# Windowed attention in fp32 by head pairs, one head in each row half of TensorE's array, with a new priority table for the list scheduler

## The chip, the cores and the metric

The kernel runs on one core of a Trainium2 chip. The metric is the device time of one execution in microseconds (us); the kernel before has a median of 611.61 us over three runs (611.47 to 611.87).

## The reference, cut to what matters

Three stages follow each other. The change is in the first one and in the order of all three.

```python
# q, k, v: 4 batches x 8 heads x 576 positions x 64
scores = q @ k.T / 8 - slope[h] * |rel|      # rel = query position - key position
scores = where((rel >= 0) & (rel < 128), scores, -1e9)
attn = softmax(scores)                       # exp, sum, divide by (sum + 1e-9)
x = attn @ v                                 # heads side by side: 4 x 576 x 512
# stage 2, gMLP: h = gelu(x @ w_in), halves u and v; v = layernorm(v);
#   x = x + (u * (w_sg @ v + b_sg)) @ w_out
# stage 3, RWKV channel mix: out = sigmoid(xr @ w_r) * (relu(xk @ w_k)^2 @ w_v)
#   xk, xr: mixes of each position with the one before it
```

All inputs and results are fp32 (the weights of the two later stages arrive as 64 bit words and are decoded on the chip).

## The kernel before, in words

**Attention.** A query tile is 128 positions; because of the window it needs 256 keys, the first tile 128. A head has four whole tiles (i = 0 to 3) and a last one of 64 queries (i = 4). `s_bank` computes score tiles into PSUM, two tiles to a bank, and the tag `s` has two banks. Heads 0 to 7 (`PLAIN_S`) multiply in fp32, with the contraction of 64 padded to all 128 rows of the array; the trace writes each fp32 matmul as two MATMUL passes. Heads 8 to 31 use fp32r instead: `prep_head` splits q and k into a rounded part and a rest (tiles QK and KL), both parts of q lie one above the other in the 128 rows, and two fp32r matmuls (`s<-QK`, `s<-KL,QK`) make a tile. `s_tile` adds the mask and takes the row maximum on DVE (one custom operation out of PSUM, the tile p and nmax), ACT takes the exponential with its sum, and after a head's last tile the sums are inverted (sum, rin) and the five tiles are scaled on DVE, POOL or ACT.

Then p is transposed on TensorE. From head `FOLD` = 16 on, a tile's two key halves are first added, so that four transposes do (`tf`), and `keep` takes the triangles apart again afterwards; the last queries of two heads take two more with 64 rows (`tf4`). Heads 0 to 15 need seven transposes of 128x128 and three small ones with 64 rows (`t`). `av_step` multiplies v by a pair's transposed tiles: one head in each column half of the array (64 columns each, `a<-pf,rawv`). The last 64 queries follow apart in `a4_step`, whose matmuls go into the half empty bank of a later head's last score tile (`s<-pf,rawv`). Copies to x and the split into xg (a cast and a subtraction for each 128 of 512 columns) end the stage.

**gMLP** (`moe1`) makes v tiles (5 x 12 matmuls, `d<-w_in_t,xg`), u tiles (`d<-xg,w_in_t`), the position mix (`d<-w_sg_t,vhl`) and the output (`d<-gg,w_out_t`), all in fp32r in three passes over split operands. `merge` interleaves batch b's gMLP with batch b+1's attention; the first batch's attention has nothing to lie under, so a first stretch ends where the first `d` matmul starts. There, matmuls of constant data (`wps<-tri`, `K.filler`) stand where the planner expects TensorE to wait. Stage 3 (`phase2`: `d<-xk,wk`, `rps`, `vps`) follows.

**What sets the order.** Every operation is recorded with its estimated cost on each engine that may do it. `Rec.rank` gives it a latest start, and the table `PRI` shifts that by the label of the written tile and the engines; `Rec.schedule` is a list scheduler that runs the engines against these numbers, chooses the engine (biases in `ENG`) and so writes out each engine's fixed instruction order, DMA issues on SP among them. Nothing is reordered at run time.

Of the kernel before, what the change touches and what calls it, by code (L numbers as in the profile page):

```python
# [20 lines left out]
P = 128  # L21
# [12 lines left out]
    ("vsg", "dve"): -4000, ("w_in_t", "act/dve/pool"): 33000, ("w_sg_t", "act/dve/pool"): -17000, ("x", "act/dve"): 4000, ("xg", "dve/pool"): -13000,  # L34
}
ENG = {
    ("KL", "dve/pool", "pool"): 68000, ("QK", "act/dve", "dve"): 17000, ("QK", "dve/pool", "dve"): 43500, ("p", "dve/pool", "dve"): -2000,
    ("p", "dve/pool", "pool"): -14000, ("p", "dve/pool/act", "act"): 1000, ("p", "dve/pool/act", "dve"): 45000, ("pf", "act/dve", "dve"): 5000,
    ("pf4", "act/dve", "act"): -36000, ("vhl", "act/dve/pool", "dve"): 13000, ("w_in_t", "dve/pool", "dve"): 2000,
    ("w_out_t", "dve/pool", "dve"): -19000, ("w_sg_t", "act/dve/pool", "dve"): -9000, ("wk", "dve/pool", "dve"): 17000,  # L40
    ("xg", "dve/pool", "dve"): 4000,
}
NWARM = 10
FOLD = 16
FM = (1, 1)


def EARLY(n, i):
    return False


PLAIN_S = (0, 1, 2, 3, 4, 5, 6, 7)
PLAIN_A = range(32)
ODD = (1, 3, 5, 7)
# [72 lines left out]
class Op:  # L127
    __slots__ = ("i", "alts", "deps", "outs", "indeg", "ready", "lst", "nominal", "rdy", "start", "end", "eng", "lat", "key", "lab", "cnt", "astart", "aend", "abusy", "w0", "pe", "port")


class Rec:
# [9 lines left out]
    SPAN, DUTY = 3400.0, 0.7  # L141
# [55 lines left out]
    def link(self, nbufs):  # L197
        ops = self.ops
        self.nb = nbufs
        for (pool, tag), tl in self.tags.items():  # L200
# [3 lines left out]
            for k in range(1, len(tl)):  # L204
# [6 lines left out]
                if prev is not first:  # L211
                    first.deps.add(prev)
# [7 lines left out]
        for o in ops:  # L220
            o.outs = []
# [311 lines left out]
def attn_gmlp_rwkv_kernel(  # L533
# [91 lines left out]
    def plain_s(n):  # L625
        return n in PLAIN_S

# [648 lines left out]
```

## Time and profile before

| | |
|---|---|
| median of 3 runs | 611.61 us (611.47 to 611.87) |
| the profiled execution: its own time, its span | 611.09 us, 609.4 us |
| PE busy in the span | 594.2 us (98%) |
| DVE, ACT, POOL busy | 453.1 us (74%), 340.1 us (56%), 204.3 us (34%) |
| chain that ended last | PE 81%, DVE 11%, ACT 5% |
| granted TensorE clock, mean | 0.999 |

The span runs from the first instruction to the last. A matmul's record is longer than the time that it takes up in a stream, since matmuls are pipelined: what one costs is the distance between the starts of two neighbours, and the text uses that throughout.

### The profile page before, as it was taken

The page shows a single profiled execution, that of the slowest core. Times are in us where ns is not written, and L with a number is a line of the kernel's source. Part 1 is how long each engine was busy: PE and PEld are TensorE (multiplying, and loading weights), DVE is VectorE, ACT ScalarE, POOL GpSimd, SP SyncE. Part 2 cuts the span into 40 slices and gives each one's busy share as a digit, 9 for nine tenths or more (in the row PEclk, how much of TensorE's full clock was granted, in tenths as well). Part 3 has the DMA queues.
Part 4 walks back from the last instruction along what each step waited for, and adds up shares of the span by engine and source line. Part 5 has one row for each costly group of instructions (what it writes and reads, how often), then busy time and mean ns, then how long its engine had stood idle before and what let it go on. Part 6 is the DMA issues. An engine that isn't in the chain of part 4 may idle for free.

```text
span 609.4 us, 10294 instructions
## 1 busy us (share of the span) xinstructions
PE 594.2 (98%) x3593; PEld 502.9 (83%) x3593; DVE 453.1 (74%) x1199; ACT 340.1 (56%) x859; POOL 204.3 (34%) x348
## 2 busy tenths in 40 slices
PE   8898999999999999999999999999999999999997
PEld 4566889998789997899889988787888887888896
DVE  5989999899999889988498998892592249226122
ACT  5898888686777767874166456532521432234031
POOL 5587672437667555673053330000000001000000
PEclk9999999999999999999999999999999999999999
DMA  8974413325131323100352427414002000000100
GB/s 305 331 214 143 154 59 98 120 89 200 40 101 54 124 65 137 40 23 13 112 207 70 139 93 268 134 35 122 17 18 86 1 0 37 34 2 0 53 18 34
DMA packets 25332, 57.74 MB, mean 95 GB/s; under 512 B 4416, under 2 KB 13120, under 8 KB 24768
## 3 DMA queue, kind: packets, MB, share of 16 engines
q1 hardware_dynamic: 25280, 57.09, 28.4%
q8 instruction: 28, 0.46, 0.3%
q14 instruction: 24, 0.20, 0.1%
HBM read 47.63 MB, written 9.45 MB: 94 GB/s over the span
## 4 chain that ended last, share of the span: by engine, by line
PE 81%; DVE 11%; ACT 5%; issue 1%; DMA 1%; POOL 0%; SPq 0%; DVEq 0%; ACTq 0%; POOLq 0%
PE d L398 46%; PE vps L398 15%; PE rps L398 7%; PE s L398 6%; PE a L398 4%; PE t L406 2%; PE tf L406 2%; ACT p L420 1%; ACT wdec L591 1%; DVE p L718 1%; DVE wdec L476 1%; DVE w_v_t L440 1%; DVE mt L476 1%; DMA rawqk<-in_qk_dram 1%; ACT p L503 1%
## 5 line engine op out<-in xcount | busy, mean ns | idle before, releaser
L398 PE MATMUL d<-xk,wk 128*128 128x512 f32 (+1 forms) x480 | 105.3, 368 | 0.0
L398 PEld LDWEIGHTS d<-xk,wk 128*128 128x128 f32 x480 | 84.7, 188 | 16.1
L398 PE MATMUL vps<-w_v_t,k2h 128*128 128x512 f32 x288 | 94.1, 396 | 0.3 <-DVE r L440 0.3
L420 ACT ACTIVATE p<-p,nmax 128x256 f32<-128x256 f32 (+3 forms) x160 | 76.6, 480 | 27.5 <-DVE nmax L718 26.9
L420 ACT ACTIVATE rl<-d 128x512 f32<-128x512 f32 (+1 forms) x40 | 22.1, 554 | 81.2 <-PE d L398 76.4
L398 PE MATMUL d<-w_sg_t,vhl 128*128 128x288 f32 x448 | 66.4, 298 | 0.0
L398 PEld LDWEIGHTS vps<-w_v_t,k2h 128*128 128x128 f32 x288 | 54.2, 188 | 13.7 <-DVE r L440 1.0
L718 DVE CUSTOM_DVE_ANT_0 p<-s,mask 128x256 f32<-128x256 f32 (+3 forms) x160 | 60.1, 381 | 6.8 <-PE s L398 6.2
L398 PEld LDWEIGHTS d<-w_sg_t,vhl 128*128 128x128 f32 x448 | 60.8, 188 | 0.7 <-issue 0.2
L398 PE MATMUL d<-w_in_t,xg 128*128 128x512 f32 (+1 forms) x240 | 61.2, 399 | 0.0
L398 PE MATMUL vps<-w_v_t,k2l 128*128 128x512 f32 x144 | 57.0, 396 | 0.0
L430 DVE CAST k2h<-rl 128x512 fp32r<-128x512 f32 (+1 forms) x31 | 12.1, 391 | 59.9 <-ACT rl L448 59.8
L398 PE MATMUL d<-xg,w_in_t 128*128 128x288 f32 x384 | 56.7, 298 | 0.0
L398 PE MATMUL d<-gg,w_out_t 128*128 128x288 f32 x384 | 56.6, 297 | 0.0
L398 PE MATMUL rps<-w_r_t,xr 128*128 128x512 f32 x216 | 54.5, 390 | 1.4 <-ACT r L420 1.4
L398 PEld LDWEIGHTS d<-xg,w_in_t 128*128 128x128 f32 x384 | 52.1, 188 | 1.0
L398 PEld LDWEIGHTS d<-gg,w_out_t 128*128 128x128 f32 x384 | 52.1, 188 | 0.5 <-issue 0.2
L398 PEld LDWEIGHTS d<-w_in_t,xg 128*128 128x128 f32 (+1 forms) x240 | 40.9, 177 | 10.9
L398 PEld LDWEIGHTS rps<-w_r_t,xr 128*128 128x128 f32 x216 | 40.2, 188 | 10.1 <-ACT r L420 1.8
L496 POOL TENSOR_SCALAR p<-p,rin 128x128 f32<-128x128 f32 (+4 forms) x73 | 39.5, 552 | 23.8 <-DVE rin L741 17.9
L440 DVE TENSOR_TENSOR r<-vps,r 128x512 f32<-128x512 f32 x18 | 12.4, 689 | 43.9 <-PE vps L398 43.8
L496 POOL TENSOR_SCALAR mt<-xc,mus 128x512 f32<-128x512 f32 (+3 forms) x9 | 8.8, 978 | 84.7 <-ACT xk L428 49.5
(134 smaller groups left out, 1192.4 us busy)
## 6 DMA issues: line engine op xcount, KB each, us to landing
rawqk<-in_qk_dram SPq DMA_DIRECT2D x32, 576.0 KB, 4.0
rawv<-in_v_dram SPq DMA_DIRECT2D x32, 160.0 KB, 2.3
xs<-x SPq DMA_DIRECT2D x4, 1154.0 KB, 5.9
out_dram<-r SPq DMA_DIRECT2D x18, 256.0 KB, 2.0
st<-in_w_in_dram SPq DMA_DIRECT2D x8, 512.0 KB, 7.0
wraw<-in_w_k_dram SPq DMA_DIRECT2D x8, 512.0 KB, 3.7
wraw<-in_w_v_dram SPq DMA_DIRECT2D x8, 512.0 KB, 3.4
wraw<-in_w_out_dram SPq DMA_DIRECT2D x8, 256.0 KB, 2.6
```

Of the source, the lines that this page charges most:

```text
L398: pe.matmul(real(o), real(l), real(r), start=st, stop=sp, **ex)
L406: pe.transpose(real(o), real(i), real(d))
L420: nc.scalar.activation(real(out), real(in_), func, scale=scale, **kw)
L430: alts.append(("dve", self._dve(in_.n, not in_.ps), lambda: nc.vector.tensor_copy(real(out), real(in_))))
L440: alts.append(("dve", self._dve(out.n, False), lambda: nc.vector.tensor_tensor(real(out), real(a), real(b), op)))
L476: alts.append(("dve", cost or self._dve(out.n, False, isinstance(s, Vw)), lambda: nc.vector.scalar_tensor_tensor(real(out), real(a), real( ...
L496: alts.append(("pool", 240 + out.n if ptr else 150 + 0.83 * out.n, lambda: nc.gpsimd.tensor_scalar(real(out), real(a), real(s1), real(s2), ...
L503: alts.append(("act", self._act(a, 1), lambda: nc.scalar.mul(real(out), real(a), real(s1))))
L591: K.raw("act", K._act(hf), lambda: nc.scalar.activation(real(w), real(hf), ACTF.Prelu, scale=2.0 ** -112, alpha=-(2.0 ** 32)), [hf], [w])
L718: K.raw("dve", 70 + w / 0.96, lambda: nc.vector.tensor_tensor_reduce(out=real(pw), in0=real(si), in1=real(ma), scale=-0.125, scalar=3.0e38 ...
```

## The change

Scores are made for a pair of heads at once. q and k of one head lie in partitions 0 to 63, those of the other in 64 to 127, and each head's fp32 matmuls use one half of the array's rows and one PSUM bank of their own; the fp32r split (`prep_head`, QK, KL) is gone. The last 64 queries of both heads are stacked into one tile of 128 partitions (`s_last`, with a mask of its own, mask4): one maximum, one exponential, one scaling and one transpose serve both. `FOLD` goes from 16 to 8. The product for the last queries (now the tile a4) stands right behind the pair's `a`. The first v tile of the first gMLP is opened in the first stretch (`v_first`). Buffers for p grow from 12 to 20, for v from 3 to 4. The link between two tiles of one tag becomes pure order (`order`, `next`), not a wait. `PRI`, `ENG`, `NWARM` and `DUTY` get new numbers.

```diff
-    ("KL", "dve/pool"): 6000, ("QK", "act/dve"): -8000, ("QK", "dve/pool"): -46000, ("bn", "dve"): 4500, ("bsg2", "dve"): 5000,
...
+    ("wraw", "sp"): -6900, ("wz", "dve"): 95500, ("x", "act/dve"): 2800, ("x", "dve"): -218300, ("x", "pool"): -900, ("xc", "sp"): 43100,
...
-NWARM = 10
-FOLD = 16
...
+NWARM = 12
+FOLD = 8
+
+PLAIN_S = ()
...
+    def load_pair(c):
+        if c >= NPR:
             return
+        b, h = divmod(2 * c, H)
+        rawqk[c] = T("raw", [P, 2, S], F32, "raw", "rawqk")
+        for j in range(2):
+            r = slice(64 * j, 64 * j + 64)
+            K.dma(rawqk[c][r], qkT[b, h + j, 0:64], 64 * 2 * S * 4)
...
+        banks = [T("psS", [P, 2, 256], F32, "s") for _ in range(2)]
         it = []
         for k, i in enumerate(ii):
-            q0, m, k0, w, c0 = q_geom(n, i)
-            s = bank[:, k, :]
-            if plain_s(n):
-                raw = rawqk[n]
-                it.append((s[:m, :w], raw[:, 0, q0:q0 + m], raw[:, 1, k0:k0 + w], True, True, {}))
-            else:
-                it.append((s[:m, :256], QK[n][:, 0, q0:q0 + m], QK[n][:, 1, k0:k0 + 256], True, False, {}))
-                it.append((s[:m, :256], QK[n][:, 0, q0:q0 + m], KL[n][:, k0:k0 + 256], False, True, {}))
+            q0 = i * P
+            k0, w = (q0 - P, 256) if i else (0, P)
+            for j in range(2):
+                r = slice(64 * j, 64 * j + 64)
+                it.append((banks[j][:, k, :w], rawqk[c][r, 0, q0:q0 + P], rawqk[c][r, 1, k0:k0 + w], True, True, {}))
         K.mm(it)
...
+    def s_last(c):
+
+        bank = T("psS", [P, 2, 256], F32, "s")
+        raw = rawqk.pop(c)
+        it = []
+        for j in range(2):
+            r = slice(64 * j, 64 * j + 64)
+            it.append((bank[r, 0, 0:192], raw[r, 0, 512:576], raw[r, 1, 384:576], True, True, SG))
+        K.mm(it)
+        s_tile(c, 2 * c, 4, bank[:, 0, 0:192], mask4[:, 2 * c % H // 2, :], 8)
...
+    def t4_step(c):
+        t = T("psT", [P, 2, 64], F32, "t", "tf4")
+        K.transposes([(t.flat(), PT.pop((2 * c, 4)), ident)])
...
+        a4b = T("psS", [P, 2, 256], F32, "s", "a4")[:, 0, 0:64]
+        AV.append(K.mm([x for y in zip(*its) for x in y] +
+                       [(a4b[r0:r0 + 64], rv[:, 3 + k, :], pf[k], k == 0, k == 1, SG) for k in range(2) for r0, rv, pf in a4]))
...
+    def v_first(a, z):
+        if not V0:
+            V0.append(T("psD", [P, 512], F32, "d"))
+        v_mms(V0[0], 0, 0, P, range(a, z))
+        return V0[0]
```

Where the instructions stand now is shown at three places. The first is PE in the middle of the program, where batch 1's gMLP lies over the scores of later heads. Before (`tf_2921` is a pair's two small transposes, `s<-pf_2945` the product for the last queries, `s<-QK` and `s<-KL,QK` the scores):

```order
L406 MATMUL tf_2921<-ident,p 128x64 x2
L398 MATMUL d<-w_sg_t,vhl 128x288 x28
L398 MATMUL s<-pf_2945,rawv 64x64 x4
L398 MATMUL d<-w_sg_t,vhl 128x288 x6
L398 MATMUL s<-QK 128x256
L398 MATMUL s<-KL,QK 128x256
L398 MATMUL s<-QK 128x256
L398 MATMUL s<-KL,QK 128x256
L398 MATMUL d<-w_sg_t,vhl 128x288 x2
L398 MATMUL s<-QK 64x256
L398 MATMUL s<-KL,QK 64x256
L398 MATMUL a<-pf,rawv 64x256 x6
```

On the same engine at a like place of the change, `tf_2376` is the one transpose of a pair's last queries, `a_2454` the product for them, and `s<-rawqk 64x192` the stacked last score tile:

```order
L431 MATMUL d<-xg,w_in_t 128x288 x30
L439 MATMUL tf_2376<-ident,p 128x128
L431 MATMUL d<-xg,w_in_t 128x288 x30
L431 MATMUL a<-pf,rawv 64x256 x6
L431 MATMUL a<-pf,rawv 64x128 x2
L431 MATMUL a_2454<-pf_2386,rawv 64x64 x4
L431 MATMUL s<-rawqk 64x192 x2
L431 MATMUL d<-xg,w_in_t 128x288 x6
L431 MATMUL s<-rawqk 128x128 x2
L431 MATMUL s<-rawqk 128x256 x2
```

The products of a pair and its last score tile now form one block, and the next pair's first score tiles, which need both banks of the tag `s`, follow six `d` matmuls later.

The second place is the start of the program on SP, which issues the DMAs one after another. Before:

```order
L508 DMA rel<-in_rel_dram 128x320
L508 DMA ident<-in_ident_dram 128x128
L508 DMA rawqk<-in_qk_dram 128x1152 x2
L508 DMA rawv<-in_v_dram 128x320
L508 DMA st_158<-in_w_in_dram 128x1024
```

And of the change:

```order
L541 DMA rel<-in_rel_dram 128x320
L541 DMA rawv<-in_v_dram 128x320 x4
L541 DMA ident<-in_ident_dram 128x128
L541 DMA rawqk<-in_qk_dram 64x1152 x2
L541 DMA st_152<-in_w_in_dram 128x1024
```

Four loads of v moved ahead of the first q and k, which are the seventh and eighth issue instead of the third.

The third place is PE at the end of the first stretch. Before, the first `d` stands behind the products of heads 6 and 7 and the scores of heads 8 and 9 (QK):

```order
L398 MATMUL a<-pf_857,rawv 64x128
L398 MATMUL s<-QK 128x256
L398 MATMUL s<-KL,QK 128x256
L398 MATMUL s<-QK 128x256
L398 MATMUL s<-KL,QK 128x256
L398 LDWEIGHTS tri
L398 MATMUL wps<-tri 128x256
L398 MATMUL s<-QK 64x256
L398 MATMUL s<-KL,QK 64x256
L398 MATMUL d<-w_in_t,xg 128x512 x6
```

In the change (`a_890` is the last product of heads 6 and 7, the first `s` row behind it the last tile of heads 8 and 9, the next two the first tiles of heads 10 and 11, and `tf` the transposes of heads 8 and 9):

```order
L431 MATMUL a_890<-pf_864,rawv 64x64 x4
L431 MATMUL s<-rawqk 64x192 x2
L431 LDWEIGHTS tri
L431 MATMUL wps<-tri 128x256
L431 MATMUL s<-rawqk 128x128 x2
L431 MATMUL s<-rawqk 128x256 x2
L431 MATMUL d<-w_in_t,xg 128x512 x3
L439 MATMUL tf<-ident,p 128x128 x4
L431 MATMUL s<-rawqk 128x256 x4
L439 MATMUL tf<-ident,p 128x128 x4
L439 MATMUL tf_996<-ident,p 128x128
L431 MATMUL d<-w_in_t,xg 128x512 x24
```

The three `d` in the middle are the last quarter of the first v tile; its other nine matmuls stand further ahead, among the scores of earlier pairs.

## Rows read from the trace of the kernel before

**Rows 1.** Stretch, its us, busy PE, PEld, DVE, ACT, POOL, clock, DMA, GB/s.

```profile
7.27:59.30 52.03, 45.99 (x325) 32.66 (x324) 45.81 (x153) 48.05 (x150) 35.29 (x48) 1.00 0.75 249
59.30:300.00 240.70, 239.37 (x1763) 211.99 (x1762) 216.57 (x622) 171.88 (x484) 130.99 (x238) 1.00 0.27 88
300.00:380.00 80.00, 80.00 (x480) 72.17 (x479) 74.19 (x143) 45.66 (x83) 26.12 (x35) 1.00 0.48 162
```

**Rows 2.** PE's waits, whole span: total us, times, longest.

```profile
PE s L398 <- DVE nmax L718: 4.3, 9, 0.8
...
PE rps L398 <- ACT r L420: 1.4, 1, 1.4
```

**Rows 3.** PE in order of time: start, us, operation, count, idle before.

```profile
20.91 1.13 PE L398 MATMUL s<-rawqk 128*128 128x256 f32 x4
21.88 0.60 PE L406 MATMUL t<-ident,p 128*128 128x128 f32 x4
...
62.56 0.28 PE L398 MATMUL s<-QK 128*128 128x256 f32 x1
...
63.02 1.56 PE L398 MATMUL d<-w_in_t,xg 128*128 128x512 f32 x6
64.42 0.28 PE L398 MATMUL s<-QK 128*128 128x256 f32 x1
...
71.06 0.81 PE L406 MATMUL t<-ident,p 128*128 128x128 f32 x6
71.80 1.66 PE L398 MATMUL d<-w_in_t,xg 128*128 128x512 f32 x6
```

**Rows 4.** PE in order of time, folded heads.

```profile
166.21 0.60 PE L406 MATMUL tf<-ident,p 128*128 128x128 f32 x4
166.57 1.03 PE L398 MATMUL d<-xg,w_in_t 128*128 128x288 f32 x6
167.44 0.28 PE L398 MATMUL s<-QK 128*64 128x256 f32 x1
...
167.68 0.96 PE L398 MATMUL d<-xg,w_in_t 128*128 128x288 f32 x6
168.57 0.33 PE L406 MATMUL tf<-ident,p 64*128 64x64 f32 x2
168.83 1.07 PE L398 MATMUL d<-xg,w_in_t 128*128 128x288 f32 x6
```

**Rows 5.** PE in order of time, around one pair's products.

```profile
177.33 0.70 PE L398 MATMUL d<-xg,w_in_t 128*128 128x288 f32 x4
177.96 0.45 PE L398 MATMUL s<-pf,rawv 128*64 128x64 f32 x8
178.24 1.69 PE L398 MATMUL a<-pf,rawv 128*64 128x256 f32 x16
179.86 0.39 PE L398 MATMUL s<-QK 128*128 128x256 f32 x1
180.08 0.28 PE L398 MATMUL s<-KL,QK 128*128 128x256 f32 x1
```

**Rows 6.** SP's DMA issues in order of time: start, us, count.

```profile
0.79 0.39 SPq L508 DMA_DIRECT2D rel<-in_rel_dram  x1
...
1.70 0.90 SPq L508 DMA_DIRECT2D rawqk<-in_qk_dram  x2
```

**Rows 7.** Chain of work that ended last, its first transfer: start, us, what.

```profile
1.70 4.23 DMA rawqk<-in_qk_dram
```

**Rows 8.** ACT in order of time, first and last piece of the first stretch.

```profile
7.27 0.40 ACT L420 ACTIVATE p<-p,nmax 128x128 f32<-128x128 f32 x1 [5.20 <-DVE nmax L718]
...
58.98 0.56 ACT L428 COPY x<-a 128x512 f32<-128x512 f32 x1
```

**Rows 9.** DVE in order of time, first stretch.

```profile
20.09 0.71 DVE L440 TENSOR_TENSOR w_in_t<-wdec,w_in_t 128x512 fp32r<-128x512 f32 x1
...
60.55 0.90 DVE L440 TENSOR_TENSOR xg<-x,xg 128x576 fp32r<-128x576 f32 x1
```

More of the change, by code (lines that the diff above doesn't have):

```diff
@@ L127 @@
 class Op:
-    __slots__ = ("i", "alts", "deps", "outs", "indeg", "ready", "lst", "nominal", "rdy", "start", "end", "eng", "lat", "key", "lab", "cnt", "astart", "aend", "abusy", "w0", "pe", "port")
+    __slots__ = ("i", "alts", "deps", "outs", "indeg", "ready", "lst", "nominal", "rdy", "start", "end", "eng", "lat", "key", "lab", "cnt", "astart", "aend", "abusy", "w0", "pe", "port", "order", "next")
 class Rec:
@@ L211, in link @@
                 if prev is not first:
-                    first.deps.add(prev)
+                    first.order.add(prev)
         for late, early in self.after.items():
@@ L220, in link @@
         for o in ops:
-            o.outs = []
+            o.outs, o.next = [], []
         for o in ops:
+            o.order -= o.deps
+            for d in o.order:
+                assert d.i < o.i
+                d.next.append(o)
             o.deps = [d for d in o.deps]
@@ L240, in rank @@
                 l = m - cost - o.lat
-            o.lst = l
+            o.lst = min([l] + [c.lst for c in o.next])
         for o in self.ops:
@@ L251, in schedule @@
         for o in ops:
-            o.indeg, o.start = len(o.deps), None
+            o.indeg, o.start = len(o.deps) + len(o.order), None
             o.rdy = {a[0]: 0.0 for a in o.alts}
@@ L351, in schedule @@
                 moved = True
+                for c in o.next:
+                    c.indeg -= 1
+                    if not c.indeg:
+                        for x in c.rdy:
+                            heapq.heappush(soon, (max(c.rdy[x], t), c.i, x))
                 for c in o.outs:
@@ L693, in s_bank @@
         K.mm(it)
+        if ii[0] == 0:
+            SUM[c] = T("st", [P, 9], F32, "sum")
         for k, i in enumerate(ii):
-            s_tile(n, i, bank[:, k, :])
-        if len(ii) == 1 and A4:
-            a4_step(bank)
-    def a4_step(bank):
-        n, it = A4.pop()
-        b, c = n // H, n % H // 2
-        K.mm([(bank[r0:r0 + 64, 1, 0:64], rv[:, 3 + k, :], pf[k], k == 0, k == 1, SG)
-              for k in range(2) for r0, rv, pf in it])
-        K.copy(x_t[b][:, c, 513:577], bank[:, 1, 0:64])
-        xsplit_later(b, c)
@@ L818, in attn_gmlp_rwkv_kernel, with av_step @@
+        K.copy(PTc[n][:, 4:7, :], t[:, 0:3, :])
+        for i in range(4):
+            PT.pop((n, i))
+    def t4_step(c):
+        t = T("psT", [P, 2, 64], F32, "t", "tf4")
+        K.transposes([(t.flat(), PT.pop((2 * c, 4)), ident)])
+        pf = T("pt", [P, 2, 2, 64], F32, "pf4")
+        K.copy(pf[:, 0], t)
+        K.keep(pf[:, 1], pf[:, 0], True, "dp")
+        K.keep(pf[:, 0], pf[:, 0], False, "dp")
+        P4[c] = pf
     SG = {"skip_group_check": True}
-    def av_step(n):
-        b, c = n // H, n % H // 2
+    def av_step(c):
+        b, ch = 2 * c // H, c % (H // 2)
@@ L852, in av_step @@
-        AV.append(K.mm([x for y in zip(*its) for x in y]))
-        A4.append((n, a4))
-        if c == 0:
+        p4 = P4.pop(c)
+        for j in range(2):
+            m = 2 * c + j
+            rv, pf = rawv.pop(m), PTc.pop(m)
+            ar = a[64 * j:64 * j + 64]
+            its.append([(ar[:, ki:min(ki + 2, 4), :], rv[:, ki, :], pf[:, ki::4, :] if fold(m) else pf[:, 2 * ki:min(2 * ki + 2, 7), :],
+                         ki == 0, ki == 3, SG) for ki in range(4)])
+            a4.append((64 * j, rv, (p4[:, 1, j, :], p4[:, 0, j, :])))
@@ L936, in v_tile @@
                 cd["v"] = T("gp", [P, 9, DM], F32R, "G", "vhl")
-            g, vhl = XG[b], cd["v"]
+            vhl = cd["v"]
             m = min(P, S - s * P)
-            ps = T("psD", [P, 512], F32, "d")[:m]
-            group(ps, [(g[:, kk, pa, s * P:s * P + m], w_in_t[:, kk, pb, DM:DF])
-                       for kk in range(NC) for pa, pb in PASS], 6)
+            if b == 0 and s == 0:
+                ps = v_first(1, NC)
+            else:
+                ps = T("psD", [P, 512], F32, "d")[:m]
+                v_mms(ps, b, s, m, range(NC))
             if b == B - 1:
@@ L1176, in attn_gmlp_rwkv_kernel @@
         a = []
-        for n in range(8 * (b + 1) + 1, 8 * (b + 2) + 1):
-            if n <= NH:
+        for n in range(4 * (b + 1) + 1, 4 * (b + 2) + 1):
+            if n <= NPR:
                 a += slot(n)
```

321 lines of the change are left out of this document (114 added, 207 removed), and 9 rows, old and new, of the table PRI.

## The prediction

> **What bounds the kernel now.** I read the stretches first, then PE's waits, then PE, ACT and DVE in order of time. In the stretches the reader is to see two regimes [rows 1]. From 59.3 us on PE never stops: 239.4 us busy of 240.7, then 80.0 of 80.0. Time is lost there only by what PE is given to do. Before 59.3 us PE is busy 46.0 of 52.0 us, fillers included, while ACT is busy 48.1 and DVE 45.8: this stretch ends when ACT and DVE have worked through the softmax of the first heads. PE's waits say the same from the other side: scores waited 4.3 us for DVE to empty their banks, and one group of stage 3 waited 1.4 us [rows 2]; no other wait is over 2 us in total. So the change is worth what it takes from PE behind 59.3 us, plus the shift of that point, plus new waits.
>
> **PE behind 59.3 us, priced.** All prices are distances between starts. An fp32r score matmul costs 0.115 us (0.46 for four [rows 3]), 0.12 with 64 queries [rows 4]. An fp32 pass of 256 columns costs 0.217: four with all rows in use take 0.97, 0.10 of it entry [rows 3]. A `d` of 512 columns costs 0.233 (six in 1.40 [rows 3]). One of 288 columns costs 0.1325: 0.87 for six behind `tf`, less the 0.075 that the first is held up [rows 4]. A 128x128 transpose costs 0.11: four take 0.36 and delay the next `d` by 0.075 [rows 4].
>
> The array's form has a price too. Two 64-row transposes in a stream of `d` [rows 4]: the six `d` ahead take 0.89, not 0.795, and those behind start late as well. Around a pair's products [rows 5], the four `d` ahead take 0.63, not 0.53; the block of `s<-pf` and `a` starts slowly (0.05); leaving it costs 0.10, and the next matmul comes after 0.22, not 0.115. In and out is 0.35, so 0.175 a change of form at columns; I take the same for row halves with fp32 loads. fp32r with 64 queries shows none of it [rows 4].
>
> *Scores.* Behind 59.3 us stand 22 heads, 11 pairs. Before, a pair takes 20 x 0.117 = 2.34 us. After, the whole tiles of each head have 128 + 3 x 256 columns in two passes, seven passes of 256 in all: 1.5 us if both row halves stream at once, and the last tile 0.32: 1.81. If the halves take turns, it is 3.62. The trace has no matmul in the lower row half. The nearest row is the product by column halves: eight fp32 matmuls, 16 passes, in 1.62 us [rows 5], where one after the other they need about 3.1. That is two at once, and in order of issue as here, so I take 1.81. One pair's first tiles move ahead of the point, so 25.7 becomes 19.3: **-6.4 us**; -6.4 + 19.3 if the halves take turns.
>
> *Transposes, with their own changes of form.* Six in a row, three of them small, take 0.74 and hold up the next `d` by about 0.09 [rows 3]; less 0.33 for the wide ones, three small ones cost 0.50. Heads 8 to 15 have those and seven wide ones each: 8 x 1.27 = 10.2 us. Heads 16 to 31 take 16 x 0.44 = 7.0, and their eight pairs' two small ones 0.46 each (0.26, 0.095 ahead, 0.11 behind [rows 4]): 3.7. After, all 24 heads are folded and a pair's small one is a wide one in the same form: 24 x 0.44 + 12 x 0.11 = 11.9. From 20.9 to 11.9: **-9.0 us**.
>
> *Other changes of form, counted in both orders.* Before 44, all by products (ten of twelve pairs have the last queries apart, so four changes; two have two). After 77, seven a pair: 5 for the scores, 2 for the products. 33 more at 0.175: **+5.8 us**. Row halves alone would thus lose: 0.53 a pair saved, 0.87 spent; what gains is the folding and the stacking around them.
>
> *First v tile.* Nine of its 12 `d` run under the first stretch, where PE has time: **-2.1 us**. If PE has none, they cost the same there and the term is 0.
>
> Sum -11.7 us (bounds: +-0.09 a change for the 77, so 7 either way).
>
> **The first stretch.** The corresponding point of the change is the start of the last three `d` of the first v tile. On SP, q and k were issued third at 1.70 us [rows 6] and landed 4.23 later [rows 7]. Issues are 0.45 apart (two in 0.90 [rows 6]); five more stand ahead, and the bytes ahead grow by 480 KB, so the second half is issued at about 3.9 and lands at about 7.1: +1.2 us, between +0.5 and +2.2 (all five issues). The change's first exponential can hardly start before 8.4, not 7.27 [rows 8].
>
> From there to the copy of the fourth pair's x, ACT worked from 7.27 to 58.98 [rows 8]. By its list, ACT loses one wide cast of QK, 4 exponentials of last tiles and 3 wide copies of p, and gains scalings, w_sg casts and two decodings: 46.2 becomes 44.1 us, about -2.3 at its busy share of 0.92. DVE, up to the fourth subtraction of xg (ends 61.4 [rows 9]), gets five weight subtractions of 0.6 from POOL (0.71 long [rows 9]), w_sg casts and subtractions, six additions of folded tiles, four half masks and five copies of p, and loses the QK and KL work of three heads (7.0): 41.5 becomes 46.0, about +5.1 at 0.88. POOL falls from 35 to about 22. The total of the three falls from 129.2 [rows 1] to about 118.6: -4.3 if all shared alike. The ends are -4.3 and +5.1; I take 0, since ACT's and DVE's bounds nearly cancel and DVE, which stretches when POOL works, gets a quieter neighbour. With the late start the point comes at 60.5, **+1.2 us**.
>
> **Waits.** A pair's first tiles need both banks of the tag `s`, and just ahead stand the last product and the last score tile, which hold both. Six `d` lie between, 0.8 us with 288 columns; PE to DVE, one maximum and back need about 0.6. An in-order DVE that is late stops PE there, and all `d` behind it. I give these places 1 us more than all such waits now [rows 2]: **+1.0**. Nothing is a bound from below: no wait at all would give -2.8.
>
> On the other side DVE is relieved: 216.6 of 240.7 us busy [rows 1] loses the split of 22 heads, so from 59.3 to 300 it will not bind. From 300 to 380 it keeps 74.2 of 80.
>
> Sum: 609.4 - 11.7 + 1.2 + 1.0 = 599.9 us of span. The profiled execution took 1.7 over its span and the median lies 0.5 above it, so **602.1 us**.
>
> **Rivals.** (1) *The row halves take turns.* For it: no row shows a lower half at work. Against it: column halves run two at once. It adds 19.3 us, and PE's slack hides what it does in the first stretch: 621. It decides once half of the overlap is lost. The Trainium skill ("TensorEngine Tiling (Array Packing)", Tiling Modes) says that different tiles load and multiply in parallel; by that the overlap is whole, and no row here shows it for rows.
>
> (2) *Evacuation becomes the bound.* Two banks filled at once must be emptied by four maxima (about 1.2 us of DVE) before the next scores. 33 handovers (three a pair) lie behind the point; the nine waits of now are 0.48 long on average [rows 2]. If each handover costs that, the change gives back 16 us instead of 1: 617. For it: DVE is at 0.90 and PE gets no second pair of banks. Against it: between a pair's groups stand 12 to 60 `d` in most places, only the six are few; DVE loses over 30 us. It decides from 0.32 us a handover. The Trainium skill warns of it ("TensorEngine Tiling (Array Packing)", Performance Considerations): tiling speeds TensorE up, not the emptying of PSUM, which can become the bottleneck. The trace of before bears that out only in its first stretch.
>
> (3) *More is gained.* The first stretch shrinks with the total work (-4.3) and waits vanish: 609.4 - 11.7 - 3.1 - 2.8 + 2.2 = 594.
>
> (4) *DVE sets the first stretch.* Its +5.1 counts whole, the first v tile then saves nothing (2.1), and waits stay as forecast: 609.4 - 9.6 + 6.3 + 1.0 + 2.2 = 609.3, up to 612 with the start at its late end: little gain or none.
>
> A measurement of this kernel cannot tell a difference within 0.2%, 1.2 us, from none.
>
> **Chances.** Forecast 0.66, own range 596 to 608; more gained 0.10; DVE first 0.09; evacuation 0.08; turns 0.07. Faster: the first two and half of the DVE case, 0.81; same: the rest of that, 0.04; slower 0.15. To leave out no more than 2 in 10, the range takes in the third case and DVE's: 592 to 612.
>
> **What would show it.** Right: in the trace after, `s<-rawqk` passes of the two heads start within some ns of each other, a whole pair's tiles taking about 1.5 us; `tf4` among `d` without 0.09 of delay; the last three `d` of the first v tile near 60; PE's waits behind it under 5 us. Wrong: passes 0.21 apart one by one (rival 1), many waits of `s` for nmax of half a us (rival 2), first maximum later than 9 us or ACT with gaps over 1 us in the first stretch (the point later than 64).

## The result, and the profile after

The changed kernel takes 607.2 us (median of six runs, 603.6 to 607.9); the kernel before took 611.7 beside it. The ratio is 0.9912, with an interval of 0.9884 to 0.9940: faster, by less than forecast (602.1), and inside the range. Its times are of two sorts, which the runs' mean granted clock tells apart: 603.6 and 604.3 us at 0.991 and 0.992, and four of 607.1 to 607.9 at 0.982 to 0.986. The kernel before has 0.999 in its profiled execution and 0.998 to 1.000 wherever it ran beside an experiment. The profiled execution is one of the first sort: 603.6 us, span 601.9.

The stretches of the changed kernel, columns as in [rows 1], the last two lines being pieces of the first:

```profile
8.96:65.40 56.44, 48.53 (x347) 32.16 (x347) 45.44 (x169) 47.11 (x150) 19.78 (x32) 0.91 0.70 196
65.40:300.00 234.60, 234.49 (x1718) 199.92 (x1718) 190.64 (x593) 135.87 (x419) 92.83 (x195) 1.00 0.23 67
300.00:380.00 80.00, 79.99 (x478) 71.94 (x477) 74.53 (x148) 48.83 (x91) 22.03 (x32) 1.00 0.45 141
...
9.00:20.00 11.00, 10.12 (x53) 6.62 (x53) 6.70 (x33) 7.34 (x24) 2.07 (x4) 0.69 1.03 304
...
50.00:60.00 10.00, 8.16 (x46) 5.47 (x46) 7.45 (x32) 7.57 (x27) 1.16 (x4) 0.83 0.62 155
```

Behind 65.4 us PE never stops, as before behind 59.3. The first window starts at the first scores; that of [rows 1] starts 1.3 us later, at the first exponential. Counted from the first scores in both kernels, the work has hardly changed (DVE 45.4 and ACT 47.1 us, against 46.2 and 48.1 before), but the stretch is 3.1 us longer (56.4 against 53.3), so both stand idle for longer, and the granted clock is no longer 1.00. PE's waits, columns as in [rows 2]:

```profile
PE s L431 <- DVE nmax L723: 3.9, 4, 1.4
PE s L431 <- DMA rawqk<-in_qk_dram: 2.7, 1, 2.7
PE t L439 <- ACT p L536: 1.8, 1, 1.8
```

They all lie in the first stretch: the waits for nmax before 54 us, and stage 3's wait for ACT [rows 2] is gone. PE in order of time, in the first stretch (answers to [rows 3]):

```profile
8.96 2.39 PE L431 MATMUL s<-rawqk 64*128 64x128 f32 x8 [2.66 <-DMA rawqk<-in_qk_dram]
12.19 2.42 PE L431 MATMUL s<-rawqk 64*128 64x256 f32 x8 [0.84 <-DVE nmax L723]
...
20.03 1.14 PE L431 MATMUL s<-rawqk 64*128 64x256 f32 x8
...
27.50 1.00 PE L431 MATMUL s<-rawqk 64*128 64x128 f32 x8 [0.88 <-DVE nmax L723]
...
30.84 0.66 PE L439 MATMUL t<-ident,p 128*128 128x128 f32 x4 [1.80 <-ACT p L536]
...
48.18 2.54 PE L431 MATMUL a<-pf,rawv 128*64 128x256 f32 x24
...
54.82 2.59 PE L431 MATMUL d<-w_in_t,xg 128*128 128x512 f32 x6
...
61.41 1.97 PE L431 MATMUL a<-pf,rawv 128*64 128x256 f32 x24
...
65.40 1.33 PE L431 MATMUL d<-w_in_t,xg 128*128 128x512 f32 x3
```

The first scores start at 8.96 instead of 5.97 us. The same group takes 2.42 us at 12.19 and 1.14 at 20.03: the clock stood at its lower level (1.2 GHz) in the first case. Up to the point it stood there for 10.2 us in all, 6.8 from 9.1 and 3.4 from 53.4. The corresponding point, forecast at 60.5, is 65.4. DVE's longest wait for weights in this stretch, with four maxima in order behind it:

```profile
47.34 0.31 DVE L463 CAST w_sg_t<-wraw 128x288 fp32r<-128x288 f32 x1 [1.80 <-DMA wraw<-in_w_sgT_dram]
```

And PE where batch 1's gMLP lies over the scores (answers to [rows 4, 5]):

```profile
194.94 1.06 PE L431 MATMUL d<-w_sg_t,vhl 128*128 128x288 f32 x6
195.93 0.93 PE L431 MATMUL s<-rawqk 64*128 64x128 f32 x8
196.79 1.85 PE L431 MATMUL d<-w_sg_t,vhl 128*128 128x288 f32 x12
198.47 1.04 PE L439 MATMUL tf<-ident,p 128*128 128x128 f32 x8
199.44 1.14 PE L431 MATMUL s<-rawqk 64*128 64x256 f32 x8
200.50 3.18 PE L431 MATMUL d<-w_sg_t,vhl 128*128 128x288 f32 x22
...
207.74 0.27 PE L439 MATMUL tf<-ident,p 128*128 128x128 f32 x1
207.76 4.22 PE L431 MATMUL d<-gg,w_out_t 128*128 128x288 f32 x30
```

From start to start a pair's four whole tiles take 0.86 + 1.06 = 1.92 us, changes of form within them included; the passes of the two heads start 6 or 7 ns apart. No group waits for its banks: six `d` take 0.99 us up to the scores, and 6 x 0.1325 is 0.80, the rest being the change of form. The 1.92 us are seven passes of 0.21, and 0.2 in each of the two groups for the change.

Where the time behind the point went, as distances between the starts of successive matmuls, summed by tile:

| us, by tile | before, from 59.3 | after, from 65.4 |
|---|---|---|
| scores | 27.8 | 25.8 |
| products | 24.3 | 22.7 |
| transposes | 16.9 | 11.9 |
| `d<-w_in_t,xg` (nine fewer) | 57.8 | 56.1 |
| all other `d` | 267.0 | 265.7 |
| `rps`, `vps` | 152.1 | 150.0 |
| sum | 545.8 | 532.2 |

So PE gains 13.6 us behind the point, the point loses 6.1, and the span falls by 7.5. The rest of the document asks what the first stretch loses, and why four of the six runs take 3.5 to 4.3 us more than the profiled one.

### The profile page after: what moved, and what is told of

It reads as the page before. It is cut to its first block, busy times and chain, and to the rows that moved or that the text cites. A ratio compares the mean times of both kernels' runs of the same rounds, so it can differ in the third digit from the quotient of the medians.

```text
span 601.9 us, 9953 instructions
## 1 busy us (share of the span) xinstructions
PE 586.0 (97%) x3542; PEld 485.1 (81%) x3542; DVE 407.3 (68%) x1105; ACT 307.7 (51%) x809; POOL 188.0 (31%) x340
## 4 chain that ended last, share of the span: by engine, by line
PE 91%; DMA 3%; DVE 2%; SPq 1%; ACT 1%; issue 1%; POOL 0%; DVEq 0%; POOLq 0%
PE d L431 54%; PE vps L431 17%; PE rps L431 8%; PE s L431 6%; PE a L431 4%; PE tf L439 2%; DMA st<-in_w_in_dram 1%; DMA wraw<-in_w_sgT_dram 1%; SPq L541 1%; DMA rawqk<-in_qk_dram 1%; PE t L439 1%; DVE p L723 0%; POOL w_sg_t L475 0%; PE wps L551 0%; DVE wdec L509 0%
## 5 line engine op out<-in xcount | busy, mean ns | idle before, releaser
L431 PE MATMUL d<-xk,wk 128*128 128x512 f32 (+1 forms) x480 | 103.4, 368 | 0.0
L453 ACT ACTIVATE p<-p,nmax 128x128 f32<-128x128 f32 (+1 forms) x144 | 67.7, 472 | 22.9 <-DVE nmax L723 21.3
L529 POOL TENSOR_SCALAR mt<-xc,mus 128x512 f32<-128x512 f32 (+7 forms) x59 | 45.6, 786 | 63.3 <-DVE k2l L473 36.6
L431 PEld LDWEIGHTS vps<-w_v_t,k2h 128*128 128x128 f32 x288 | 54.1, 188 | 12.7
L431 PE MATMUL d<-w_sg_t,vhl 128*128 128x288 f32 x448 | 63.9, 298 | 0.0
L723 DVE CUSTOM_DVE_ANT_0 p<-s,mask 128x256 f32<-128x256 f32 (+1 forms) x144 | 49.9, 378 | 15.9 <-PE s L431 15.7
L431 PE MATMUL d<-gg,w_out_t 128*128 128x288 f32 x384 | 54.7, 297 | 0.0
L431 PE MATMUL s<-rawqk 64*128 64x256 f32 (+2 forms) x320 | 47.2, 388 | 7.5 <-DVE nmax L723 3.9
L492 POOL TENSOR_SCALAR_AFFINE_SELECT pf<-pf 128x512 f32<-128x512 f32 (+2 forms) x78 | 41.0, 537 | 34.3 <-ACT pf L461 28.7
L431 PE MATMUL rps<-w_r_t,xr 128*128 128x512 f32 x216 | 50.9, 390 | 0.0
```

Of the source, the lines that this page charges most:

```text
L431: pe.matmul(real(o), real(l), real(r), start=st, stop=sp, **ex)
L453: nc.scalar.activation(real(out), real(in_), func, scale=scale, **kw)
L492: nc.gpsimd.affine_select(out=real(out), in_=real(in_), pattern=[[0, rows], [sgn, n]], compare_op=cmp, fill=0.0, base=0, channel_multiplie ...
L529: alts.append(("pool", 240 + out.n if ptr else 150 + 0.83 * out.n, lambda: nc.gpsimd.tensor_scalar(real(out), real(a), real(s1), real(s2), ...
L723: K.raw("dve", 70 + w / 0.96, lambda: nc.vector.tensor_tensor_reduce(out=real(pw), in0=real(s), in1=real(ma), scale=-0.125, scalar=3.0e38, ...
```

## The experiments

All are made from the changed kernel. The planner's orders are kept, but for E8; `relay` takes one operation out of its engine's order and puts it so many places further back (negative: ahead). A tuple names engine, label of the written tile, which one, places. Only E2 and E6, with E9 to E12 that are built on E6, add work: matmuls of constant data. A point is read in the one profiled execution of each kernel, and these differ in the clock too: up to the point it stood at the lower level for 10.2 us in the changed kernel, E6 and E10, 13.7 in E1, E2, E4 and E5, 17.1 in E7 and E9, 23.9 in E3, 3.4 in E12 and not at all in E11.

**E1.** q and k of the first pair second and third on SP.

```diff
+    order = relay(R.schedule(), (("sp", "rawqk", 0, -5), ("sp", "rawqk", 1, -5)))
```

> The changed kernel with one thing moved: on SP the first pair's q and k are issued second and third again, ahead of the four loads of v; every other order stays. Theory (the late point of the changed kernel, 65.4 us instead of the forecast 60.5, comes from a start that is 3.0 us late, 8.96 instead of 5.97, and from the half clock behind that idle time): first scores at 6.0 to 6.5, granted clock 1.00 from there, start of the last three d of the first v tile at 60 to 62, time 598 to 600.5, and no runs near 607. Rival (the sum of ACT's, DVE's and the DMAs' work sets the end of the first stretch, the start only shifts idle time): first scores early, but the point stays behind 64 and the time at 602.5 or more.

Measured: 604.4 us (602.3 to 606.4), ratio 0.9892 [0.9873, 0.9912]. The first scores start at 6.71, the point is at 65.9. ACT in order of time says why:

```profile
8.00 0.40 ACT L453 ACTIVATE p<-p,nmax 128x128 f32<-128x128 f32 x1 [5.94 <-DVE nmax L723]
...
10.20 0.67 ACT L625 ACTIVATE wdec<-st 128x512 f32<-128x512 f32 x1 [1.71 <-DMA st<-in_w_in_dram]
10.78 0.49 ACT L453 ACTIVATE p<-p,nmax 128x256 f32<-128x256 f32 x1
...
16.40 0.68 ACT L625 ACTIVATE wdec<-st 128x512 f32<-128x512 f32 x1 [1.28 <-DMA st<-in_w_in_dram]
```

The second instruction of ACT decodes a weight tile, and stands in order before its transfer while exponentials wait behind it. The early start alone does not bring the point forward, as the rival has it. The full clock that the theory asked for did not come with it: the clock fell at 13.5 us, behind a wait of PE of 1.9 us, so this run does not part the start from the clock.

**E2.** Twice the warm-up matmuls.

```diff
-    K.mm([(wps, wz[:, 0:128], wz, True, True, {})] * NWARM)
+    w = K.mm([(wps, wz[:, 0:128], wz, True, True, {})] * NWARM)
+    e, cost, go, n = w.alts[0]
+    w.alts = [(e, cost, lambda: (go(), go()), 2 * n)]
```

> The changed kernel with 24 instead of 12 warm-up matmuls of constant data, 12 x 0.217 us longer, so that PE is busy until q and k land; order and issues stay. It tells the clock from the late landing. Theory: first scores still near 8.96, but at the full clock (two groups of eight passes take about 1.1 instead of 2.4 us); the point 1 to 2 us earlier, at 63.5 to 64.5; time 601.5 to 603, and runs near 607 rare or none. Rival (the half clock at the start is hidden behind DVE and ACT): clock full, point at 65 or later, times still between 603.6 and 607.9.

Measured: 605.9 us (604.5 to 608.0), ratio 0.9916 [0.9900, 0.9932]; point 67.7. The first two groups of scores take 1.11 and 1.47 us, so the clock is up; yet the point is later. The clock fell elsewhere instead, behind two waits (PE in order of time):

```profile
27.93 1.00 PE L431 MATMUL s<-rawqk 64*128 64x128 f32 x8 [0.88 <-DVE nmax L723]
...
31.27 1.11 PE L439 MATMUL t<-ident,p 128*128 128x128 f32 x4 [1.80 <-ACT p L536]
...
33.03 1.70 PE L439 MATMUL t<-ident,p 128*128 128x128 f32 x7
```

The changed kernel has the same two waits, and in its profiled run the seven `t` behind them take 1.12 us. So the rival's numbers came, but not for its reason: the clock stood at the lower level for longer than in the changed kernel, and what the half clock at the start costs by itself stays open.

**E3, E4.** Five w_sg_t instructions of DVE later; E4 with E1's move as well.

```diff
+    order = relay(R.schedule(), (("dve", "w_sg_t", 2, 4), ("dve", "w_sg_t", 6, 5), ("dve", "w_sg_t", 5, 5),
+                                 ("dve", "w_sg_t", 4, 5), ("dve", "w_sg_t", 3, 5)))
```

> The changed kernel with five small w_sg_t instructions of DVE moved a few places back, behind the maxima in front of which they wait for a weight transfer (1.8 us at 47.3, 0.7 at 52.2); all else stays. Theory (a DVE that stands in order behind a weight transfer is what stops scores and products between 45 and 57 us, with the second fall of the clock): the four maxima start at about 45.7 instead of 47.57, no half clock near 54, point at 62.5 to 64, time 600.5 to 602.5 in its faster runs. Rival (the maxima are not what PE waits for there): point at 65 or later, time unchanged at 603.6 to 607.9.

> The changed kernel with both moves, q and k first on SP and the w_sg_t instructions of DVE later. Theory: the two gains add up: granted clock at 1.00 nearly throughout, point at 58.5 to 60.5, time 596.5 to 599, all runs within 0.3%. Rival: not more than the better of the two alone.

Measured: E3 610.9 us (608.3 to 612.0), ratio 0.9991 [0.9978, 1.0005], point 73.6; E4 608.2 (607.3 to 609.7), 0.9957 [0.9943, 0.9971], point 70.4. Both theories fall, and the loss shows the mechanism. SP's issues in the changed kernel, in order of time:

```profile
41.62 10.39 SPq L541 DMA_DIRECT2D wraw<-in_w_sgT_dram  x6
52.11 1.01 SPq L541 DMA_DIRECT2D rawv<-in_v_dram  x2
53.17 1.11 SPq L541 DMA_DIRECT2D rawqk<-in_qk_dram  x2
54.32 0.60 SPq L541 DMA_DIRECT2D wraw<-in_w_sgT_dram  x1
```

SP's issues in E3:

```profile
45.13 13.52 SPq L541 DMA_DIRECT2D wraw<-in_w_sgT_dram  x6
...
60.96 0.60 SPq L541 DMA_DIRECT2D wraw<-in_w_sgT_dram  x1
```

And DVE in E3, the instruction that takes what the last of these issues brings:

```profile
65.37 0.31 DVE L463 CAST w_sg_t<-wraw 128x288 fp32r<-128x288 f32 x1 [3.46 <-DMA wraw<-in_w_sgT_dram]
```

Six issues take 10.4 us, since a transfer goes into one of two buffers (`wraw`) that a cast and a subtraction must empty first. Later casts delay SP (13.5 us), SP delays the last transfer, and DVE stands before it for 3.5 us with softmax work behind it.

**E5.** Those casts, and two subtractions, on POOL (the list names what is handed to it).

```diff
+    order = relay(R.schedule(), (), [("w_sg_t", k) for k in (4, 8, 10, 14, 15, 16, 17, 18)])
```

> The changed kernel with the six casts and two subtractions of w_sg_t that stand in DVE's order put on POOL, at the place in POOL's order where they were to start; all other orders stay. The runs before showed that an earlier start and a full clock at the start do not move the point, and that later casts on DVE moved it from 65.4 to 73.6 us: a ring of two weight buffers, of which SP's next issues wait for the casts and DVE waits for the transfers. Theory (DVE's waits in order for those transfers, 2.5 us in the stretch, are what the softmax loses there): DVE waits for no weight transfer, point at 62 to 64, times 600 to 603 in the faster runs. Rival (the ring itself, not who works it, holds SP's issues and with them the next q, k and v): POOL waits instead, point at 65 or later, time not under 603.

Measured: 607.1 us (606.6 to 610.8), ratio 0.9937 [0.9923, 0.9951]; point 70.5 in the profiled run, the longest of the six. POOL now waits 9.9 us for the transfers (four times, longest 4.7). The rival is right: who works the ring matters less than when SP can issue. DVE waits for no weight transfer any more, as the theory asked, and nothing is gained by it.

**E6.** 6 and 11 more constant matmuls ahead of the two waits at 27.5 and 30.8 us (`fill` lists the constant matmuls in order of issue; two of them are issued 7 and 12 times).

```diff
+    for k, n in ((28, 7), (32, 12)):
+        e, cost, go, c = fill[k].alts[0]
+        fill[k].eng = (e, cost, lambda go=go, n=n: [go() for _ in range(n)], c * n)
```

> The changed kernel with more matmuls of constant data where PE waited 0.9 us (27.5) and 1.8 us (30.8): 6 and 11 more of 0.11 us. Theory (the changed kernel's two sorts of time, 603.6 to 604.3 and 607.1 to 607.9, are runs in which the clock does not fall or falls behind those two waits, as it fell at 30.5 for 6.8 us in the run with more warm-up matmuls): no half clock between 26 and 45, no times over 606, median 603 to 604.5. Rival (the fall of the clock is somewhere else or does not matter): both sorts of time again.

Measured: 603.6 us (603.1 to 604.4), ratio 0.9883 [0.9868, 0.9898]; point 65.2; the second sort of time is gone. The stretch from 26 to 36 us in E2:

```profile
26.00:36.00 10.00, 7.32 (x50) 5.39 (x46) 7.59 (x23) 8.73 (x23) 6.33 (x9) 0.73 0.81 233
```

The same stretch in E6:

```profile
26.00:36.00 10.00, 7.96 (x65) 5.74 (x64) 7.77 (x27) 9.31 (x27) 5.46 (x9) 1.00 0.81 235
```

And in the changed kernel's profiled run, with the waits unfilled:

```profile
26.00:36.00 10.00, 7.32 (x59) 5.02 (x59) 8.33 (x28) 9.84 (x27) 6.89 (x10) 1.00 0.74 201
```

The clock is 0.73 in E2, 1.00 in E6, and 1.00 in this execution too. That its fall behind these waits is what most of the changed kernel's own runs pay is inferred, none of them having been profiled: from this run, and from their mean clock (as an estimate, the 6.8 us that the clock was down in E2 lower the mean of a run by 0.006, and the two sorts are 0.005 to 0.010 apart).

**E7.** A group's scores head by head instead of in turns.

```diff
-        for k, i in enumerate(ii):
-            ...
-            for j in range(2):
+        for j in range(2):
+            for k, i in enumerate(ii):
```

> The changed kernel with the score matmuls of a group issued head by head (both tiles of the one row half, then both of the other) instead of in turns; same matmuls, same places. It prices the overlap of the row halves. Theory (the halves overlap because neighbours in the order of issue lie in different halves): passes of one half 0.21 apart, only the pass at the border overlaps, so a group of two 256-column tiles takes 1.06 + 3 x 0.21 = 1.7 us and one with a 128-column tile 0.4 more: about 1.05 a pair, 11 pairs behind the point, +11 us, time 613 to 619. Rival (each half has a queue of its own and overlaps whatever the order): no change, 603.6 to 607.9.

Measured: 606.9 us (606.2 to 608.9), ratio 0.9942 [0.9921, 0.9963], the second sort of time; its clock is at 0.76 from 26 to 36. PE behind the point takes 531.9 us, as with the turns, and so does a group:

```profile
199.63 0.93 PE L431 MATMUL s<-rawqk 64*128 64x128 f32 x8
200.50 1.85 PE L431 MATMUL d<-w_sg_t,vhl 128*128 128x288 f32 x12
```

The passes of the two halves still start in pairs, 13 ns apart. The rival is right in the time: the overlap does not hang on the order of issue within a group. (Whether a queue for each half is the reason, no run shows.)

**E8.** The first v tile in one piece.

```diff
-                ps = v_first(1, NC)
+                ps = v_first(0, NC)
...
-            v_first(0, 1)
```

> The changed kernel without the early begin of the first v tile: its 12 matmuls stand together behind the first stretch; the planner makes its orders anew from the same numbers. Theory (nine of the 12 lie in time that PE has anyway in the first stretch): PE behind the first d takes 2.1 us more, the first d stands near 63 to 66, time 1.5 to 4 us above the changed kernel's 603.6 to 607.9. Rival (the nine cost as much where they stand, at half clock 0.43 us each between 54.8 and 57.2): first d two us earlier than the last three d were, time unchanged or lower.

Measured: 613.7 us (610.9 to 615.9), ratio 1.0057 [1.0036, 1.0077]. The time says little, for the planner made other orders: PE waits 1.4 and 3.9 us at 90 and 96 us, and the next products take 3.77 instead of 1.97. What can be read is the price in front. The first `d` starts at 62.20, and the same place of the changed kernel, ahead of the scores that now stand before the last three `d`, is at 64.07. So the early nine cost about 1.9 us where they stand, six of them at half clock, and save 1.7 behind the point by the table above. That is the rival's sign, read across two plans.

**E9.** E6, and three maxima of DVE (of last score tiles) ahead of weight work.

```diff
+    order = relay(R.schedule(), (("dve", "p", 18, -1), ("dve", "p", 28, -2), ("dve", "p", 39, -3)))
```

> The kernel of the filled holes with three of DVE's maxima (those of the last score tile of three pairs, which free a bank that PE waits for) one, two and three places further ahead, in front of weight work: at 27.1, 40.4 and 52.9 us they stood behind 0.6, 2.1 and 1.5 us of it. Theory (what the first stretch loses is weight work that stands in the order of DVE ahead of softmax work for which PE waits, and the clock that falls in those waits): PE's waits of 1.4 us at 39.4 and 0.85 at 52.5 shrink to under 0.5, no half clock between 20 and 65, point at 61.5 to 63.5, time 600 to 602. Rival (ACT's share, 9.7 to 9.9 us busy of each ten between 20 and 40, holds the stretch, so that DVE's order moves only waits): point 64.5 or later, time 603 to 604.4 as with the filled holes alone.

Measured: 606.6 us (604.9 to 607.7), ratio 0.9918 [0.9903, 0.9933]; point 69.2. The wait at 39.4 is gone, but PE, now earlier, meets the last w_sgT transfer: 2.25 us of DVE's time at 60.7, after which the clock falls. The theory fails, and the time is above the rival's range too; the rival's mechanism fits, since the waits only moved: PE now waits 1.61 us for ACT up to 43.6.

**E10.** E9 with E1's move, and the first decodings behind the first pair's softmax.

```diff
+        ("sp", "rawqk", 0, -5), ("sp", "rawqk", 1, -5), ("act", "wdec", 0, 8),
+        ("dve", "w_in_t", 0, 2), ("dve", "wdec", 1, 5), ("dve", "wdec", 0, 5),
```

> The kernel with the maxima earlier, and also q and k first on SP as in the run with the early start, with the first weight decoding on ACT (1 instruction) and DVE (3) behind the first pair's softmax, where it no longer waits for its weights ahead of it. Theory (the early start was worth nothing by itself because ACT and DVE stood in order behind a weight tile that landed at 10.2 us): first scores at 6.7, ACT without a gap over 0.6 us up to its first decoding, point 1.5 to 3 us earlier than with the maxima alone, time 597.5 to 600. Rival (the weights land no earlier, all 16 DMA engines being busy to 28 us, so that the decodings further on wait instead): the gain is under 1 us.

Measured: 604.9 us (604.0 to 605.4), ratio 0.9895 [0.9883, 0.9908]; point 67.2. Each stage is earlier than in E9 (the second piece of the v tile at 51.6 instead of 54.1) until ACT and DVE stand before the ring's last transfers. ACT in order of time:

```profile
59.05 0.43 ACT L625 ACTIVATE wdec<-wraw 128x256 f32<-128x256 f32 x1 [1.81 <-DMA wraw<-in_w_out_dram]
```

DVE there:

```profile
58.69 0.31 DVE L463 CAST w_sg_t<-wraw 128x288 fp32r<-128x288 f32 x1 [2.53 <-DMA wraw<-in_w_sgT_dram]
```

And PE behind it:

```profile
59.86 0.47 PE L439 MATMUL tf<-ident,p 128*128 128x128 f32 x1 [2.53 <-DVE pf L463]
...
61.33 3.68 PE L431 MATMUL a<-pf,rawv 128*64 128x256 f32 x24
```

PE's wait costs twice: 2.53 us, and 1.71 more for the products behind it at half clock. The point moved by 2.0 us, as the theory has it, the time by only 1.7 and not to 600.

**E11.** E10 with these two issues ahead of the next pair's v, q and k.

```diff
+        ("sp", "wraw", 11, -4), ("sp", "wraw", 12, -4),
```

> The kernel of the early start with two issues on SP moved: the last w_sgT and the first w_out transfer stand ahead of the next pair's v, q and k instead of behind them. In the run before, DVE stood 2.5 us (to 58.7) and ACT 1.8 us (to 59.1) in order before these two transfers, issued at 53.6 and 54.4, and the clock fell there for 6.8 us. Theory (in the first stretch the time goes where ACT or DVE stands in order before a transfer that SP issued late): both waits under 0.7 us, no half clock behind 50, point at 63.5 to 65, time 600.5 to 602.5. Rival (the transfers land no earlier, since the two buffers they go into are freed late): waits as before, time 604 to 605.4.

Measured: 600.7 us (600.2 to 602.6), ratio 0.9836 [0.9822, 0.9850], with the point at 61.6. The stretch from 50 to 66 us:

```profile
50.00:66.00 16.00, 14.49 (x97) 9.05 (x94) 14.52 (x60) 13.76 (x45) 5.35 (x12) 1.00 0.72 192
```

And PE in order of time, at the point:

```profile
61.61 1.32 PE L431 MATMUL d<-w_in_t,xg 128*128 128x512 f32 x3
```

The theory holds for the time, and the point is even earlier than it asked: two issues of SP, moved by four places, are worth 4.3 us in the median. DVE's wait is gone and ACT's is down to 0.88 us. Not all of the 5.6 us at the point is theirs. E11 leads by 1.3 us already at the second piece of the v tile (50.3 against 51.6), before either transfer could have landed, because the clock fell in E10 behind a wait that E11 has as well. PE in E10:

```profile
17.32 0.66 PE L439 MATMUL t<-ident,p 128*128 128x128 f32 x4 [2.42 <-POOL p L529]
17.90 2.07 PE L431 MATMUL s<-rawqk 64*128 64x256 f32 x8
```

PE in E11:

```profile
17.45 0.66 PE L439 MATMUL t<-ident,p 128*128 128x128 f32 x4 [2.42 <-POOL p L529]
18.04 1.13 PE L431 MATMUL s<-rawqk 64*128 64x256 f32 x8
```

From that piece to the point it is 15.6 us in E10 and 11.3 in E11. Against the kernel before, this version is faster than the changed kernel: 0.9836 and 0.9912.

**E12.** E11 with more weight work behind the first softmax.

```diff
-        ("dve", "w_in_t", 0, 2), ("dve", "wdec", 1, 5), ("dve", "wdec", 0, 5),
+        ("act", "wdec", 1, 3), ("pool", "w_in_t", 0, 5),
+        ("dve", "w_in_t", 0, 9), ("dve", "wdec", 1, 8), ("dve", "wdec", 0, 8),
```

> The kernel with the two issues moved on SP, and with the second weight decoding of ACT behind three scalings of p, and what the first decoded weight tile asks of DVE and POOL behind the first pair's softmax. In the run before, ACT stood 3.2 us (13.4 to 16.5) before the second weight tile and PE 2.4 us behind it. Theory as before (each such wait that is taken out is won): PE's wait at 17.4 under 0.7 us, point 1.5 to 2 us earlier, near 59.7, time 598.5 to 599.5. Rival (the weights' landing itself is now the limit: ACT waits 0.5 us at 26.3 for the sixth tile already, and will wait longer if it comes there earlier): the wait goes to the tiles of 24 to 27 us, gain under 0.7 us, time 599.8 to 601.

Measured: 600.6 us (598.3 to 602.1), ratio 0.9816 [0.9795, 0.9838], not told apart from E11; point 62.5. ACT now waits for weights 3.38 us at 17.9, 1.00 at 19.6 and 0.58 at 22.1. PE's wait at 17.4 is gone, and one of 0.9 us at 21.6 has come. The rival's time came, though its waits lie earlier than the 24 to 27 us that it named. The landing of the weights as the limit fits, with the DMA engines at a share of 1.03 from 8 to 26 us; but PE also waited 1.5 and 0.8 us for q and k up to 13.3 and 14.5, and the clock fell there for 3.4 us, which it did not in E11.

## Why the prediction was off by 5 us, step by step

The forecast for an execution like the profiled one was 601.6 us, the median standing 0.5 above it. PE's part came out 2.9 better, the first stretch 4.9 worse: 603.6, as measured. So two errors of opposite sign hide much of each other, and that the forecast lies so near a run of the first sort is in part luck. The median has 3.6 more, from the clock as far as E6 shows it.

**PE behind the point: right, and somewhat better.** Forecast -11.7 and +1.0 for waits; measured -13.6. Scores, transposes and changes of form were to give -9.6 together. Scores, products, transposes and the other `d` give -2.0 - 1.5 - 5.0 - 1.3 = -9.8. In that stand 1.1 us of waits of scores (below), so the work itself gives -8.7, and the sum nearly holds. Its split can't be checked row by row, since part of a change's price falls on the `d` beside it. The price of a change was too low rather than too high: between `d`, a block of scores is entered 0.09 late, its first pass takes 0.10 more, leaving it costs 0.10 and the next `d` 0.10, 0.39 in and out, where 0.35 was taken. The Trainium skill ("TensorEngine Tiling (Array Packing)", Key Properties) says that a change of the tiling mode drains TensorE; the trace agrees in so far as a change in and out costs 0.39 us here. `tf4` among `d` costs a transpose's own time and no delay beyond it, as forecast: thirty `d` and one `tf` take 4.17 us from 207.74 to the next block; 30 x 0.1325 is 3.98, the next block is entered 0.09 late, and 0.10 is left for the `tf`.

**The row halves overlap whole**, so rival 1 is out: 6 or 7 ns between the heads, seven passes of 256 columns a pair. E7 adds that not even the order of issue matters. The Trainium skill ("TensorEngine Tiling (Array Packing)", Tiling Modes) says that different tiles load and multiply in parallel; the trace agrees, with these 6 or 7 ns, for rows too.

**Waits behind the point: +1.0 forecast, -2.8 measured.** Before, PE waited there, beside the 1.4 us of stage 3 in [rows 2]:

```profile
PE s L398 <- DVE nmax L718: 1.1, 3, 0.5
PE vps L398 <- DVE r L440: 0.3, 1, 0.3
```

After, no wait is left behind the point. No handover of the banks costs anything, PE being busy 234.49 of 234.60 us: rival 2 is out. Stage 3's waits went as well: `rps` and `vps` fall by 2.1 us. That was the case with no wait, for which the prediction gave -2.8.

**First v tile: -2.1 forecast behind the point, -1.7 measured by its tile, but paid in front** (1.9 us by E8, read across two plans). The prediction's other case, a term of 0, is nearer.

**The first stretch is the step that failed: +1.2 forecast, +6.1 measured.** Its work was not larger than forecast: DVE 46.0 forecast and 45.4 measured, POOL about 22 and 19.8. (That DVE's figure is met so nearly is in part luck: the prediction counted 41.5 for the kernel before, where [rows 1] has 45.8 busy, and the rise that it forecast is not there.) Two things were wrong. The late start was mis-sized. Start, us, what, in the chain of work that ended last:

```profile
3.58 5.33 DMA rawqk<-in_qk_dram
```

The second half, for which the prediction gave 3.9 and 7.1, was issued at 4.19 and landed at 9.66, 5.5 us later and not 3.2. Four v transfers of 160 KB stand ahead, 640 KB where the prediction counted 480. The scores started on the first half, 3.0 us late and not 1.2. And the other 3 us, by which the stretch is longer from the first scores on, were not in the sum at all. The sum weighed work by busy share and left no room for instructions that stand in order before a transfer, nor for a clock that falls while PE waits for them. The prediction named the signs of this (first maximum later than 9 us, gaps of ACT over 1 us, a point later than 64), and all three came: 10.96 us, 9.2 and 0.9 to 1.7, 65.4. Its rival with a point so late was DVE's amount of work (rival 4: 59.3 + 6.3 = 65.6). That it names the measured point is luck, since DVE's work did not grow (45.4 us from the first scores to the point, 46.2 before).

**What the cause is.** Shown by the waits: weight work in the orders of ACT and DVE, and weight issues in that of SP, stand where their transfers have not landed, and PE waits behind them. Moving one thing did not bring the point forward (E1 65.9, E3 73.6, E9 69.2), because the next wait stood a little further on; with the start, the first decodings, three maxima, two holes and two issues changed together, the point is 61.6, 1.1 from the forecast, and the time 600.7, 1.4 below it (E11). So it is these orders together, and not the amount of work, that cost 3.8 of the 4.9 us.

Not shown is that the waits' own length makes the loss. From the first scores to the point PE waits 9.5 us in E11 and 7.2 in the changed kernel, and ACT and DVE wait 5.8 and 3.4 us for weights. What sets E11 apart is a start 2.3 us earlier and a clock that never falls up to the point, where the changed kernel has 10.2 us at the lower level. No run has the clock up in the whole first stretch and the rest as it was, so start, waits and clock are not parted. That the clock's fall in PE's waits of 0.9 and 1.8 us makes the second sort of time, 3.6 us in the median, is what E6 shows in four runs without that sort.

## What to carry to other kernels

In a stretch that several engines fill in fixed orders, adding up busy time is not enough: go through each engine's order for instructions that need a transfer, and ask when its issue can leave SP, whose own order stands behind buffers that others must empty. Taking out a single such wait gave nothing in E1, E3 and E9 and looked like a refutation; the next wait has to be looked for in the new trace, and the granted clock has to be compared before two profiled runs are. And a gap of PE in a part of the program that is not bound by PE still costs, if the matmuls behind it run at half clock on the path.

## What the runs showed of the hardware that was not expected

- The granted clock fell to its lower level in or just behind PE's gap of 1.8 us, with one of 0.9 us ahead of it, in E1 to E4 (0.83, 0.73, 0.74 and 0.83 from 26 to 36 us, down for 3.4 or 6.8 us), and did not in the profiled run of the changed kernel with the same gaps (1.00). In E5 and E7 it fell there too (0.73 and 0.76), but the gaps were longer, 1.5 to 1.6 and 2.4 us. With seventeen more constant matmuls there it stayed at 1.00 in the profiled run of E6, and all four of its runs have a mean clock of 0.988 to 0.993.
- Behind the same gap of 2.42 us near 15 to 17.4 us the clock fell in E10 (0.79 from 14 to 22 us) and not in E11 (1.00).
- At the lower level a group of 24 products takes 3.68 us instead of 1.97, and eight score passes 2.42 instead of 1.14.
- Matmuls in the two row halves start 6 or 7 ns apart when issued in turns (195.9 to 200.2 us) and 13 ns apart when issued half by half (E7, 199.6 to 200.2 us).
- A block in row halves between full ones costs 0.39 us on top of its passes (195.9 to 197.0 us).
